# Retention and two gated layers on one core: parity by parity matmuls, an earlier scaling of chunk 4, tables in two parts

## The chip, the cores and the metric

One NeuronCore of a Trainium2 chip runs the whole program. The metric is the device time in microseconds (us) of one execution, from the first to the last instruction and what lies around them; shorter is better. The engines are TensorE (PE in the rows; PEld is its weight load), VectorE (DVE), ScalarE (ACT), GpSimd (POOL) and SyncE (SP, which issues most DMAs).

## The reference

Three stages follow one another. Inputs are float32; the output is [3072, 512].

```
state = gamma * state + k_t (outer) v_t          # 4 sequences, 8 heads, 768 steps, head size 64
y_t   = scale * q_t . state                      # gamma = 1 - 2^(-5-h), one for each head h
x     = y, heads side by side                    # [3072, 512]
h     = x @ w_in ; x = (h * sigmoid(1.702 h)) @ w_out            # 512 -> 2048 -> 512
x     = (sigmoid(x @ w_gate) * (x @ w_val)) @ w_out2             # 512 -> 1536 -> 512
```

The weights arrive in float64 and are turned into float32 on the core.

## The kernel before

**The recurrence as chunks.** The steps are cut into chunks of 128 (24 chunks, s = 0 to 23, six for each of four sequences; c = s mod 6). For each chunk the 8 heads are held as four pairs (`hp`), two parities each (`i`): parity 0 lies in partitions 0 to 63, parity 1 in 64 to 127. A chunk has four inputs of 256 KB, called Q, K, V and KN (k with time along the partitions). Its work is:

- `emit_qs(s)`: q times the decay table `dq_sb`, on POOL, L111. `emit_vs(s)`: v times the row `dv_sb[c]`, on POOL, L117.
- `emit_scores(s)`: eight float32 matmuls k.qs (L138), one for each parity and pair. A parity uses one half of the rows of the array and writes a PSUM bank of its own. After the four of one parity, DVE multiplies its bank with the triangle `tri` into `A` (L141).
- `emit_y(s)`: where c > 0 four matmuls with the state `R` (L173, the whole array); then eight matmuls of the values, vs.A (L180), again one for each parity and pair. Here a parity uses one half of the array's columns; both write the same bank, each its half of the partitions. DVE scales the bank by `dg_sb` (L186); then `halves()` takes it apart: ACT writes the upper part `xh` (L190), DVE the rest `xl` (L191).
- `emit_update(s)`, not where c = 5: eight matmuls kn.vs of half the width (L160) into the bank `st`, four for a parity, which again uses half of the columns. After each parity ACT copies its half of `st` into `R` (L165).

A float32 matmul of the program stands as two MATMUL records in the trace, so the eight matmuls of the scores are 16 records.

`burst(s)` runs emit_y(s), emit_update(s), emit_scores(s+1) and the halves of s, in that order on PE (for s = 3 there are no scores, and the halves come ahead of the update).

**The first gated layer.** `units` is the list of pieces (block of 512 tokens, slice of 128 hidden features). A unit i runs `proj` (12 matmuls of 512 columns, L262 to L264, into a bank "h"), `gated` (ACT sigmoid L272, DVE product L273; later units also ACT L278 and DVE L285), and `emit_out` of unit i-2 (L361 or L365 to L367). Bursts 0 to 3 run ahead of unit 0; bursts 4 to 23 are put into chosen units between the unit's `proj` and its `emit_out`. There are three "h" banks, taken in turn by `proj`, by emit_y and by the two parities of the scores. So in a burst of units the second bank of the scores is the one that the unit's own `proj` wrote, and it has to wait for L273; and the next `proj` takes the bank that emit_y wrote, and waits for `xl`.

**Weights.** `stage` issues DMAs of float64 tiles (L209, 512 KB each, four buffers), `convert` makes float32 of one: ACT L225 and L227, DVE L232 and L235, POOL L245. `split_for(i)` then makes the two parts wh (ACT L254) and wl (POOL L255; from unit 24 on DVE) that `proj` of unit i reads. Unit 0 and the bursts ahead of it need the first two of these.

**Order.** The body stands under a manual schedule: on every engine instructions run as the code emits them, and DMAs of the SP queue are issued in that order too, each waiting for its buffer. `load_next(s, ...)` loads inputs of a chunk into the pool `in_p` of 8 tiles. `dv_sb`, `dc_sb` and `dg_sb` are the small tables; DVE makes their later columns by multiplying the ones before (L693, 5 times, L695, 4 times).

The second gated layer (L390 on) follows and isn't touched.

Of the kernel before, what the change touches and what calls it, by code (L numbers as in the profile page):

```python
# [13 lines left out]
ALU = mybir.AluOpType  # L14

P = 128
D = 64
# [3 lines left out]
KC = DM // P  # L21
# [3 lines left out]
def retention_moe_moe2(  # L25
# [12 lines left out]
    nc = tc.nc  # L38
    NSTEP = qkv.shape[0]
    CPB = 6  # L40
# [36 lines left out]
    dv_sb = const.tile([P, CPB, H], F32, name="dv_sb")  # L77
    dc_sb = const.tile([P, H], F32, name="dc_sb")
    dg_sb = const.tile([P, CPB - 1, KC], F32, name="dg_sb")
# [10 lines left out]
    Q, K, V, KN = range(4)  # L90
# [8 lines left out]
    def load_next(s, *parts):  # L99
        for i in parts:  # L100
            if s < NSTEP and i not in in_t.get(s, {}):
                load_in(s, i, in_p, "in")

    qs_t, vs_t = {}, {}

    def emit_qs(s, engine=nc.gpsimd):

        if s < NSTEP:
            qs_t[s] = at_p.tile([P, KC, C], F32, name="qs", tag="qs")
            q = in_t[s][Q].rearrange("p (a i) -> p a i", a=KC)  # L110
            engine.tensor_tensor(out=qs_t[s], in0=q, in1=dq_sb, op=ALU.mult)  # L111
# [15 lines left out]
    def att_bank(name):  # L127
        banks.rotate(-1)
        return psum_tile(banks[-1], (P, 4, C))

    def emit_scores(s):

        k = in_t[s][K].rearrange("p (a j) -> p a j", a=KC)
        bank = [att_bank("sc") for _ in range(2)]
        for i in range(2):
            p = slice(D * i, D * (i + 1))
            for hp in range(KC):
                nc.tensor.matmul(bank[i][:, hp, :], k[p, hp, :], qs_t[s][p, hp, :], start=True, stop=True)  # L138
            A = a_p.tile([P, 4, C], F32, name="A", tag="A")
            A_t[s, i] = A  # L140
            nc.vector.tensor_tensor(  # L141
                out=A, in0=bank[i], in1=tri.unsqueeze(1).to_broadcast([P, KC, C]), op=ALU.mult
            )
# [3 lines left out]
    def emit_update(s):  # L147


        c = s % CPB  # L150
        if c == CPB - 1:
            return
        if c == 0:
            state[s // CPB] = psum_tile("st", (P, KC, P))
        st = state[s // CPB]
        kn, vs = in_t[s][KN], vs_t[s]
        for i in range(2):
            for hp in range(KC):
                h = 2 * hp + i
                nc.tensor.matmul(  # L160
                    st[D * i:D * (i + 1), hp, :D], kn[:, D * h:D * (h + 1)], vs[:, h, :],
                    start=(c == 0 and hp == 0), stop=True, skip_group_check=True,
                )
            a, b = D * i, D * (i + 1)
            nc.scalar.copy(R[(s + 1) % 2][a:b, :, a:b], st[a:b, :, :D])  # L165

    def emit_y(s):

        c = s % CPB
        bank = att_bank("y")  # L170
        if c > 0:
            for hp in range(KC):
                nc.tensor.matmul(  # L173
                    bank[:, hp, :], R[s % 2][:, hp, :], qs_t[s][:, hp, :],
                    start=(hp == 0), stop=False, skip_group_check=True,
                )
        for i in range(2):
            for hp in range(KC):
                h = 2 * hp + i
                nc.tensor.matmul(  # L180
                    bank[D * i:D * (i + 1), hp, :], vs_t[s][:, h, :], A_t[s, i][:, hp, :],
                    start=(c == 0 and hp == 0), stop=True, skip_group_check=True,
                )
        if c > 0:
            g = dg_sb[:, c - 1, :].unsqueeze(2).to_broadcast([P, KC, C])
            nc.vector.tensor_tensor(out=bank, in0=bank, in1=g, op=ALU.mult)  # L186
        xh, xl = (x[:, :, s % 4 * C:(s % 4 + 1) * C] for x in x_t[s // 4])

        def halves():
            nc.scalar.copy(xh, bank)  # L190
            nc.vector.tensor_tensor(out=xl, in0=bank, in1=xh, op=ALU.subtract)  # L191

        return halves
# [10 lines left out]
    def stage(n=1):  # L204

        for _ in range(min(n, len(to_stage))):
            ph, f, k = to_stage.popleft()
            t = cv_p.tile([P, 512], U64, name="w64", tag="w64", bufs=4)
            nc.sync.dma_start(out=t, in_=(w1 if ph == "1" else w2)[f, k])  # L209
            staged.append((ph, f, k, t))  # L210
# [81 lines left out]
    def burst(s):  # L292

        if s % 4 == 0:
            alloc_x(s // 4)
        halves = emit_y(s)
        if s == 3:
            halves()
        emit_update(s)
        if s + 1 < NSTEP and s != 3:  # L300
            emit_scores(s + 1)
        if s != 3:
            halves()
        for t in (in_t, qs_t, vs_t):
            t.pop(s, None)
# [351 lines left out]
    with tc.manual_schedule():  # L657
# [7 lines left out]
        for t in range(1, 4):  # L665
            for i in (Q, K, V, KN):
                load_in(t, i, wraw_p, "wraw")
                if (t, i) == (1, K):
                    nc.sync.dma_start(out=dg_sb[:, 0, :], in_=dg)
            if t != 2:  # L670
                stage()
        stage(2)
        load_next(4, Q, K, V, KN)
        nc.gpsimd.memset(tri, 1.0)
        nc.gpsimd.affine_select(
            out=tri, in_=tri, compare_op=ALU.is_ge, fill=0.0, base=0, pattern=[[1, C]], channel_multiplier=-1
# [12 lines left out]
        emit_scores(0)  # L689
        emit_vs(0)  # L690
        nc.vector.tensor_tensor(out=dc_sb, in0=dc_sb, in1=dc_sb, op=ALU.mult)
        for c in range(1, CPB):
            nc.vector.tensor_tensor(out=dv_sb[:, c, :], in0=dv_sb[:, c - 1, :], in1=dc_sb, op=ALU.mult)  # L693
        for c in range(1, CPB - 1):
            nc.vector.tensor_tensor(out=dg_sb[:, c, :], in0=dg_sb[:, c - 1, :], in1=dg_sb[:, 0, :], op=ALU.mult)  # L695
        first = second = None
        for t in range(4):
            if t < 3:
                emit_qs(t + 1)
            burst(t)  # L700
            if t == 0:
                load_next(5, Q, K, V, KN)
                first = convert(1)
                first[0]()
            elif t == 1:
                first[1]()
            elif t == 2:
                first[2]()
                second = convert(1)
                second[0]()  # L710
            if t < 3:
                emit_vs(t + 1)
            if t == 2:
                split_for(0)
        second[1]()
        second[2]()
        split_for(1)
        stage(2)
# [5 lines left out]
        for i, (b, f) in enumerate(units):  # L724
            if b == len(blocks1) - 1 and f == 0:
                assert not staged and not to_stage
                right.close()
                open_early()
                xs = prep_x(0)
                load_chain(0)  # L730
            first = staged and staged[0][0] == "1"
            conv, conv2 = ([lambda: None] * 3 for _ in range(2))
            if first:
                conv = convert(1)
                if i < FH:
                    conv2 = convert(1)
            elif staged and (5 * i) // 8 > (5 * (i - 1)) // 8:
                conv = convert(1)
            xh, xl = x_t[b]
            n = blocks1[b][1]  # L740
            if 0 < i < FH:
                split_for(i + 1)
            conv[0]()
            conv[1]()
            if i < FH:
                conv[2]()
            hb = psum_tile("h")
            proj(hb, w_t.pop((i, 0)), xh, xl, n)
            if i >= FH:
                split_for(i + 1)  # L750
            split_out(i + 1)
            if i == len(units) - 1:
                split_out(i + 2)
            g_t[i] = gated(hb, n, i < WHOLE)
            gated_lo(g_t[i], n)
            if i == 0:
                emit_qs(4)
                emit_scores(4)
                emit_vs(4)
                load_next(6, Q, K)  # L760
                emit_qs(5)
                banks.clear()
                banks.append("h")
            if i in bursts:
                burst_and_next(bursts[i])
            if i >= FH:
                conv[2]()
            stage(4 - len(staged))
            for step in conv2:
                step()  # L770
            pend.append(i)
            while pend and i - pend[0] >= DEPTH:
                emit_out(pend.popleft())
            next(xs, None)
            if b == len(blocks1) - 1:
                if f == 9:
                    sums(0)
                elif f in (11, 13):
                    split_chain(0, f == 13)()
# [144 lines left out]
```

## Time and profile before

| | us |
|---|---|
| three runs of the kernel: median (lowest to highest) | 1217.59 (1216.28 to 1217.83) |
| the execution that was profiled | 1216.4 |
| its span, first to last instruction | 1214.7 |
| PE busy in it | 1189.9 (98%) |
| DVE, ACT, POOL busy | 661.3, 573.5, 570.0 |

A row of a timeline gives the start in us from the span's start, the time from the first start to the last end, engine, line, operation, output<-inputs, their shapes and the count of merged instructions; in brackets the idle time of the engine just before, and what ended it. A MATMUL record is longer than the engine's time for it, since matmuls overlap in the pipeline: what one costs in a row of many is read from start to start. [...]

### The profile page before, as it was taken

What the parts mean: (1) busy time and instruction counts of PE and PEld (TensorE: products, weight loads), DVE (VectorE), ACT (ScalarE), POOL (GpSimd) and SP (SyncE); (2) the same over time, 40 slices, a digit from 0 to 9 for tenths busy, and PEclk for the clock granted to TensorE, in tenths of its full rate; (3) what the DMA queues carried; (4) which work ended last, traced back from release to release, by engine and by line L of the source; (5) the groups of instructions that cost most, each with busy time, mean ns of one, the idle gap of its engine ahead of it and who ended that gap; (6) DMA issues with size and microseconds to landing.
All of it is one profiled execution on the core that took longest, in us unless ns stands there. A gap on an engine that the chain in (4) does not pass through costs nothing.

```text
span 1214.7 us, 16082 instructions
## 1 busy us (share of the span) xinstructions
PE 1189.9 (98%) x5910; PEld 979.7 (81%) x5910; DVE 661.3 (54%) x904; ACT 573.5 (47%) x996; POOL 570.0 (47%) x443
## 2 busy tenths in 40 slices
PE   7799999999999999999999999999999999999998
PEld 7666888888888888888788888888888888888887
DVE  5665555455445544644565545458545458535454
ACT  3445664444555554545545534355535254625251
POOL 3665774434433543333455443438544348534340
PEclk9899999999999999999999999999999999999999
DMA  8565343633324434310300321114311123311111
GB/s 304 171 193 173 98 163 122 208 113 131 113 92 143 134 115 125 130 52 28 105 25 18 114 61 44 61 45 146 103 53 53 52 66 132 98 52 53 53 35 70
DMA packets 62431, 122.96 MB, mean 101 GB/s; under 512 B 6800, under 2 KB 16272, under 8 KB 62352
## 3 DMA queue, kind: packets, MB, share of 16 engines
q1 hardware_dynamic: 61632, 121.01, 30.6%
q8 instruction: 46, 0.75, 0.3%
q10 hardware_dynamic: 720, 0.92, 0.2%
q14 instruction: 33, 0.27, 0.1%
HBM read 97.79 MB, written 24.12 MB: 100 GB/s over the span
## 4 chain that ended last, share of the span: by engine, by line
PE 95%; DVE 1%; ACT 1%; DMA 1%; issue 0%; POOL 0%; SPq 0%; DVEq 0%; ACTq 0%; POOLq 0%
PE pa L512 16%; PE pd L512 8%; PE h L262 7%; PE h L264 7%; PE h L263 7%; PE acc L365 7%; PE acc L367 6%; PE acc L366 6%; PE po L636 4%; PE po L634 4%; PE po L635 4%; PE pb L512 4%; PE h L138 3%; PE acc L361 2%; PE h L180 2%; PE st L160 1%
## 5 line engine op out<-in xcount | busy, mean ns | idle before, releaser
L255 POOL TENSOR_TENSOR wl<-wraw,wh 128x512 fp32r<-128x512 f32 x112 | 154.1, 1381 | 293.8 <-ACT wh L254 279.7
L262 PE MATMUL h<-xh,wh 128*128 128x512 f32 x384 | 153.6, 400 | 1.6 <-DVE xl L191 1.5
L273 DVE TENSOR_TENSOR sg<-h,sg 128x512 f32<-128x512 f32 x88 | 60.8, 691 | 170.2 <-ACT sg L272 170.2
L264 PE MATMUL h<-xh,wl 128*128 128x512 f32 x384 | 149.8, 390 | 0.1
L263 PE MATMUL h<-xl,wh 128*128 128x512 f32 x384 | 149.8, 390 | 0.0
L365 PE MATMUL acc<-gh,wh 128*128 128x512 f32 x352 | 138.8, 394 | 0.0
L367 PE MATMUL acc<-gl,wh 128*128 128x512 f32 x352 | 137.1, 390 | 0.0
L366 PE MATMUL acc<-gh,wl 128*128 128x512 f32 x352 | 137.1, 389 | 0.0
L254 ACT CAST wh<-wraw 128x512 fp32r<-128x512 f32 x184 | 107.8, 616 | 38.6 <-PE acc L367 35.4
L504 POOL TENSOR_TENSOR ol<-raw,oh 128x768 fp32r<-128x768 f32 x36 | 66.9, 1859 | 124.7 <-ACT oh L501 124.7
L272 ACT ACTIVATE sg<-h 128x512 f32<-128x512 f32 x88 | 52.5, 597 | 131.7 <-PE h L264 131.4
L512 PE MATMUL pa<-xoh,oh 128*128 128x512 f32 x288 | 112.7, 391 | 0.2 <-ACT u L571 0.2
L512 PE MATMUL pa<-xol,oh 128*128 128x512 f32 x288 | 112.1, 389 | 0.0
L512 PE MATMUL pa<-xoh,ol 128*128 128x512 f32 x288 | 112.1, 389 | 0.0
L285 DVE TENSOR_TENSOR gl<-sg,gh 128x512 fp32r<-128x512 f32 x88 | 69.5, 790 | 60.4 <-ACT gh L278 60.4
L624 POOL TENSOR_TENSOR wol<-wor,woh 128x512 fp32r<-128x512 f32 x36 | 57.1, 1586 | 83.2 <-ACT woh L623 80.1
L278 ACT CAST gh<-sg 128x512 fp32r<-128x512 f32 x88 | 54.6, 621 | 71.3 <-DVE sg L273 71.3
L262 PEld LDWEIGHTS h<-xh,wh 128*128 128x128 f32 x384 | 72.3, 188 | 19.0 <-issue 3.3
L263 PEld LDWEIGHTS h<-xl,wh 128*128 128x128 f32 x384 | 72.4, 189 | 16.6 <-issue 1.9
L264 PEld LDWEIGHTS h<-xh,wl 128*128 128x128 f32 x384 | 72.3, 188 | 15.7 <-DVE wl L255 0.5
L634 PE MATMUL po<-woh,g2h 128*128 128x512 f32 x216 | 84.0, 389 | 0.0
L635 PE MATMUL po<-wol,g2h 128*128 128x512 f32 x216 | 84.0, 389 | 0.0
(136 smaller groups left out, 2622.6 us busy)
## 6 DMA issues: line engine op xcount, KB each, us to landing
w<-in_w_dram SPq DMA_DIRECT2D x68, 512.0 KB, 3.7
in_t<-in_qkv_dram SPq DMA_DIRECT2D x93, 256.0 KB, 4.0
raw<-w2d SPq DMA_DIRECT2D x72, 256.0 KB, 3.1
w2d<-cva SPq DMA_DIRECT2D x36, 256.0 KB, 2.2
wor<-w2d SPq DMA_DIRECT2D x36, 256.0 KB, 2.6
out_dram<-ost SPq DMA_DIRECT2D x23, 256.0 KB, 2.0
xt<-x2d SPq DMA_DIRECT2D x18, 256.0 KB, 4.4
x2d<-ost SPq DMA_DIRECT2D x14, 256.0 KB, 2.5
```

Source lines behind the costliest of these rows:

```text
L254: nc.scalar.copy(wh, raw)
L255: lo_engine.tensor_tensor(out=wl, in0=raw, in1=wh, op=ALU.subtract)
L262: nc.tensor.matmul(bank[:, :n], wh[:, k, :], xh[:, k, :n], start=(k == 0), stop=False)
L263: nc.tensor.matmul(bank[:, :n], wh[:, k, :], xl[:, k, :n], start=False, stop=False)
L264: nc.tensor.matmul(bank[:, :n], wl[:, k, :], xh[:, k, :n], start=False, stop=(k == KC - 1))
L285: nc.vector.tensor_tensor(out=gl[:, :n], in0=sg[:, :n], in1=gh[:, :n], op=ALU.subtract)
L365: nc.tensor.matmul(a, wh[:, wc], gh[:, :n], start=st, stop=False)
L366: nc.tensor.matmul(a, wl[:, wc], gh[:, :n], start=False, stop=False)
L367: nc.tensor.matmul(a, wh[:, wc], gl[:, :n], start=False, stop=sp)
L512: nc.tensor.matmul(bank, w[:, kk], x[:, k, :], start=start and k == 0 and w is wh and x is xh, stop=stop and k == 1 and w is wl, skip_grou ...
L634: nc.tensor.matmul(bank, gh, wh, start=f == 0, stop=False)
L635: nc.tensor.matmul(bank, gh, wl, start=False, stop=False)
```

## The change

Four edits, all in the code that makes the retention.

1. In `emit_scores`, in the values of `emit_y` and in `emit_update` the loops over parity and pair are exchanged: the matmuls alternate between the parities. The DVE products of the scores and the ACT copies of the update stand behind all eight matmuls of both parities.
2. `load_next(4, Q, K)` stands ahead of two weight loads that it followed, and V and KN of chunk 4 stay behind them.
3. `emit_qs(4)`, which stood in unit 0 behind its gating, stands ahead of the POOL step of the second weight tile.
4. The small tables: `dv_sb[1]` alone is made ahead of burst 0, columns 2 and 3 (with the first two of `dg_sb`) behind burst 0, and the last two (with the last two of `dg_sb`) behind burst 1.

```diff
@@ emit_scores
+        for hp in range(KC):
+            for i in range(2):
+                p = slice(D * i, D * (i + 1))
+                nc.tensor.matmul(bank[i][:, hp, :], k[p, hp, :], qs_t[s][p, hp, :], start=True, stop=True)
         for i in range(2):
-            p = slice(D * i, D * (i + 1))
-            for hp in range(KC):
-                nc.tensor.matmul(bank[i][:, hp, :], k[p, hp, :], qs_t[s][p, hp, :], start=True, stop=True)
             A = a_p.tile([P, 4, C], F32, name="A", tag="A")
@@ emit_update
-        for i in range(2):
-            for hp in range(KC):
+        for hp in range(KC):
+            for i in range(2):
                 h = 2 * hp + i
                 nc.tensor.matmul(
                     st[D * i:D * (i + 1), hp, :D], kn[:, D * h:D * (h + 1)], vs[:, h, :],
                     start=(c == 0 and hp == 0), stop=True, skip_group_check=True,
                 )
+        for i in range(2):
             a, b = D * i, D * (i + 1)
             nc.scalar.copy(R[(s + 1) % 2][a:b, :, a:b], st[a:b, :, :D])
@@ emit_y
-        for i in range(2):
-            for hp in range(KC):
+        for hp in range(KC):
+            for i in range(2):
                 h = 2 * hp + i
@@ the body
+        load_next(4, Q, K)
         stage(2)
-        load_next(4, Q, K, V, KN)
+        load_next(4, V, KN)
...
-        for c in range(1, CPB):
-            nc.vector.tensor_tensor(out=dv_sb[:, c, :], in0=dv_sb[:, c - 1, :], in1=dc_sb, op=ALU.mult)
-        for c in range(1, CPB - 1):
-            nc.vector.tensor_tensor(out=dg_sb[:, c, :], in0=dg_sb[:, c - 1, :], in1=dg_sb[:, 0, :], op=ALU.mult)
+        def factors(*cs):
+            for c in cs:
+                nc.vector.tensor_tensor(out=dv_sb[:, c, :], in0=dv_sb[:, c - 1, :], in1=dc_sb, op=ALU.mult)
+            for c in range(max(1, cs[0] - 1), cs[-1]):
+                nc.vector.tensor_tensor(out=dg_sb[:, c, :], in0=dg_sb[:, c - 1, :], in1=dg_sb[:, 0, :], op=ALU.mult)
+        factors(1)
...
             burst(t)
+            if t < 2:
+                factors(2 * t + 2, 2 * t + 3)
...
         second[1]()
+        emit_qs(4)
         second[2]()
...
-                emit_qs(4)
                 emit_scores(4)
```

On PE, burst 4 (in unit 1): the second half of the values, the update and the scores of chunk 5. The number at a name tells buffers apart; `[waits ...]` names the semaphores that the instruction waits for. Before:

```order
L180 MATMUL h_515<-A_463,vs_465 64x128 [waits DVE_49]
L180 MATMUL h_515<-A_463,vs_465 64x128 x3
L160 MATMUL st_244<-vs_465,in_t_185 64x64 [waits DMAHW3_49]
L160 MATMUL st_244<-vs_465,in_t_185 64x64 x3
L160 MATMUL st_244<-vs_465,in_t_185 64x64 [waits Activation_49]
L160 MATMUL st_244<-vs_465,in_t_185 64x64 x3
L138 MATMUL h_539<-qs_471,in_t_273 128x128 [waits DMAHW5_49,Pool_49]
L138 MATMUL h_539<-qs_471,in_t_273 128x128 x3
L138 MATMUL h_540<-qs_471,in_t_273 128x128 [waits DVE_49]
L138 MATMUL h_540<-qs_471,in_t_273 128x128 x3
```

The same place in the changed kernel, where these lines are L182, L161 and L138:

```order
L182 MATMUL h_515<-A_461,vs_465 64x128
L182 MATMUL h_515<-A_463,vs_465 64x128
L161 MATMUL st_236<-vs_465,in_t_185 64x64 [waits DMAHW3_49]
L161 MATMUL st_236<-vs_465,in_t_185 64x64 x7
L138 MATMUL h_539<-qs_471,in_t_269 128x128 [waits DMAHW5_49,Pool_49]
L138 MATMUL h_540<-qs_471,in_t_269 128x128 [waits DVE_49]
L138 MATMUL h_539<-qs_471,in_t_269 128x128
L138 MATMUL h_540<-qs_471,in_t_269 128x128
```

The wait for ACT in the middle of the update is gone, and the wait for DVE that stood in the middle of the scores stands at their second matmul.

On POOL, from the values of chunk 3 (vs, L117) through the two weight splits (wl) to the scaled q of chunk 5 (qs, L111). Before:

```order
L117 TENSOR_TENSOR vs<-in_t,dv_sb 128x512
L255 TENSOR_TENSOR wl<-wraw,wh 128x512
L245 TENSOR_TENSOR wraw<-cva,cvb 128x512
L255 TENSOR_TENSOR wl<-wraw,wh 128x512
L245 TENSOR_TENSOR wraw<-cva,cvb 128x512
L111 TENSOR_TENSOR qs<-in_t,dq_sb 128x512
L117 TENSOR_TENSOR vs<-in_t,dv_sb 128x512
L111 TENSOR_TENSOR qs<-in_t,dq_sb 128x512
```

The same place in the changed kernel (L247 and L257 are L245 and L255 of before):

```order
L117 TENSOR_TENSOR vs<-in_t,dv_sb 128x512
L257 TENSOR_TENSOR wl<-wraw,wh 128x512
L111 TENSOR_TENSOR qs<-in_t,dq_sb 128x512
L247 TENSOR_TENSOR wraw<-cva,cvb 128x512
L257 TENSOR_TENSOR wl<-wraw,wh 128x512
L247 TENSOR_TENSOR wraw<-cva,cvb 128x512
L117 TENSOR_TENSOR vs<-in_t,dv_sb 128x512
L111 TENSOR_TENSOR qs<-in_t,dq_sb 128x512
```

The scaled q of chunk 4 stands three instructions earlier, behind the first split instead of behind the second and a further weight tile.

## Rows read from the trace of the kernel before

**Rows 1.** The page: the chain that ended last, by engine.

```profile
PE 95%; DVE 1%; ACT 1%; DMA 1%; issue 0%; POOL 0%; SPq 0%; DVEq 0%; ACTq 0%; POOLq 0%
```

**Rows 2.** Waits of PE: us in total, times, longest.

```profile
PE st L160 <- ACT R L165: 11.1, 20, 1.6
```

**Rows 3.** Timeline of PE: one burst in a unit, from its values on.

```profile
217.06 1.25 PE L180 MATMUL h<-A,vs 128*64 128x128 f32 x13
...
218.15 0.27 PE L180 MATMUL h<-A,vs 128*64 128x128 f32 x1
218.16 0.28 PE L160 MATMUL st<-vs,in_t 128*64 128x64 f32 x2
...
218.37 0.27 PE L180 MATMUL h<-A,vs 128*64 128x128 f32 x1
218.39 0.34 PE L160 MATMUL st<-vs,in_t 128*64 128x64 f32 x3
219.19 0.68 PE L160 MATMUL st<-vs,in_t 128*64 128x64 f32 x8 [0.46 <-ACT R L165]
219.80 1.71 PE L138 MATMUL h<-qs,in_t 64*128 64x128 f32 x16
221.44 0.50 PE L365 MATMUL acc<-gh,wh 128*128 128x512 f32 x1
```

**Rows 4.** Timeline of PE: scores ahead of unit 0, parities in "acc" and "h".

```profile
17.80 0.82 PE L138 MATMUL acc<-qs,in_t 64*128 64x128 f32 x5
18.35 0.37 PE L138 MATMUL h<-qs,in_t 64*128 64x128 f32 x1
...
18.56 0.27 PE L138 MATMUL h<-qs,in_t 64*128 64x128 f32 x1
18.57 0.27 PE L138 MATMUL acc<-qs,in_t 64*128 64x128 f32 x1
...
18.79 0.72 PE L138 MATMUL h<-qs,in_t 64*128 64x128 f32 x5
19.43 1.16 PE L173 MATMUL acc<-qs,R 128*128 128x128 f32 x8
```

**Rows 5.** Timeline of PE: units 0 and 1.

```profile
30.25 0.40 PE L263 MATMUL h<-xl,wh 128*128 128x512 f32 x1
...
32.57 0.39 PE L264 MATMUL h<-xh,wl 128*128 128x512 f32 x1
37.84 3.09 PE L138 MATMUL acc<-qs,in_t 64*128 64x128 f32 x16 [4.88 <-POOL qs L111]
40.87 0.79 PE L262 MATMUL h<-xh,wh 128*128 128x512 f32 x1
...
44.63 1.05 PE L173 MATMUL h<-qs,R 128*128 128x128 f32 x8
...
51.58 0.47 PE L262 MATMUL h<-xh,wh 128*128 128x512 f32 x1 [1.52 <-DVE xl L191]
```

**Rows 6.** Stretches: us, busy PE, PEld, DVE, ACT, POOL (count), clock, DMA.

```profile
33.30:51.50 18.20, 11.76 (x84) 10.28 (x84) 10.08 (x15) 8.04 (x16) 12.02 (x10) 0.81 0.53 179
36.00:42.80 6.80, 4.96 (x21) 4.35 (x22) 2.48 (x5) 1.75 (x3) 4.01 (x4) 0.50 0.38 116
```

**Rows 7.** Timelines of POOL and DVE in the first 35 us.

```profile
23.30 1.04 POOL L117 TENSOR_TENSOR vs<-in_t,dv_sb 128x512 f32<-128x512 f32 x1
...
32.87 1.27 POOL L255 TENSOR_TENSOR wl<-wraw,wh 128x512 fp32r<-128x512 f32 x1 [0.73 <-ACT wh L254]
...
9.30 1.73 DVE L693 TENSOR_TENSOR dv_sb<-dv_sb,dc_sb 128x8 f32<-128x8 f32 x5
```

**Rows 8.** Timeline of DVE and PE behind the scores of a burst.

```profile
204.62 1.29 DVE L141 TENSOR_TENSOR A<-h,tri 128x512 f32<-128x512 f32 x2 [1.35 <-PE h L138]
205.82 0.68 DVE L191 TENSOR_TENSOR xl<-h,xh 128x512 fp32r<-128x512 f32 x1
...
207.92 0.39 PE L262 MATMUL h<-xh,wh 128*128 128x512 f32 x1
```

## The prediction

> **What bounds the kernel now.** I read the chain of work that ended last first: PE makes up 95% of it [rows 1], so a time that PE doesn't need is a time saved, as long as nothing else is late next. Then PE's waits [rows 2]: 20 times it stood in the middle of an update, until ACT had copied the first parity's half of `st`, 11.1 us in all, the longest 1.6. Next to that there is one idle stretch of 4.88 us before the scores of chunk 4, which waited for POOL's scaled q [rows 5]. Then the timeline of one burst, start to start [rows 3]: 217.06 to 219.80 for values and update (2.74 us), 219.80 to 221.44 for the scores (1.64).
>
> The row that matters most shows that PE can work on both halves of the array at once. In [rows 4] the scores of one parity ("acc") start at 17.80, the second parity ("h") at 18.35, when the first has some records left. From there on the two run side by side: "h" at 18.56, "acc" at 18.57. A single parity needs the same time for each record: five take 0.72 - 0.27 = 0.45 us from first to last start, 0.11 each. The same holds for halves of columns [rows 3]: a value of the second parity starts at 218.15, an update of the first at 218.16. So today each parity runs alone for about half of its time, since the other stands behind it in the queue, and the overlap is found only at the border.
>
> **Scores.** If both parities run together from the first matmul, the set lasts as long as one parity alone: from 18.35 to the next kind of matmul at 19.43, 1.08 us [rows 4], instead of 1.64 [rows 3]. That is 0.56 saved. Bursts 5 to 22 make 18 such sets: **10.1 us**. The two DVE products can no longer start while PE is on the second parity, which costs PE nothing while a unit's output matmuls follow (see the second rival).
>
> **Values and update.** A record of the values takes 0.11 (218.15 to 218.37 is two of them), the first a little more: 0.93 for the eight of a parity. An update takes 0.06 (a group of two lasts 0.28, one of three 0.34), a parity of eight 0.68 - 0.22 = 0.46 from first to last start, and the scores start 0.15 later [rows 3]. Together 0.93 + 0.46 + 0.15 = 1.54 instead of 2.74: 1.20 saved. Of this 0.62 comes from the order alone: the last update of the first parity starts at 218.39 + 0.12 = 218.51, the first of the second at 219.19, 0.68 where 0.06 would do. ACT's two copies now stand behind the update; who reads `R` is the next burst, a unit or more later. The burst shown waited 0.46; the mean of the 19 without the longest is (11.1 - 1.6) / 19 = 0.50 [rows 2], so 0.04 more. Bursts 6 to 22 without 11 and 17 are 15: 15 x 1.24 = **18.6 us**. Bursts 5, 11, 17 and 23 have values only: 217.06 to 218.37 + 0.11 is 1.42, minus 0.93 is 0.49; 4 x 0.49 = **2.0 us**.
>
> **The start, up to projection 2** (L262 at 51.58 [rows 5]), is worked out in three steps, since other engines are late there.
>
> Ahead of unit 0, PE alone would gain some 6 us in bursts 0 to 3 (three sets of scores and four updates, by the prices above, with the longest wait of 1.6). But DVE's products and weight steps lie between, and the values of chunk 3 need `vs`, which ran at 23.30 to 24.34 [rows 7] behind a weight tile on POOL. Of the tables' edit, four of the five dv_sb products (1.73 us for five, 0.35 each [rows 7]) and four smaller ones move from a time when DVE waited to places behind `xl` of bursts 0 and 1; I bound that between 0 (DVE waits there too) and 2 us. I take 3 us of gain, between 1 and 5.
>
> The scores of chunk 4 then find q ready: its POOL instruction stands ahead of one that waited for DVE, and K of chunk 4 is loaded before two weight tiles that nobody reads until unit 0. Projection 0 goes on at 0.232 a matmul (30.25 to 32.57 is ten) and ends at 32.80; the scores take 1.08; projection 1 can start at 33.9 instead of 40.87: 7.0. Its third matmul needs `wl`, done at 32.87 + 1.27 = 34.14 [rows 7], just in time. [...]
>
> So PE would be 11 us ahead at 44.63, and burst 4 would add its own 1.8 and the wait of 1.52 for `xl`. There I let DVE decide: it had 10.08 us of work between 33.30 and 51.50 [rows 6], the queue up to `xl` of chunk 4, and starts on it about 3 us earlier, at 30.3. Without any pause it is through at 40.4, and projection 2 starts at 40.6 instead of 51.58: 11. DVE waits for PE once or twice on the way, and PE idles while it waits, which may bring the lower clock back: I take **10 us**, between 6 (four or five us of such pauses) and 13 (the first step at its best).
>
> **The sum.** 10.1 + 18.6 + 2.0 + 10 = 40.7. The profiled execution took 1216.4, which gives 1175.7; it lies 1.2 under the median of the runs, so on the median's footing 1177. Its own range is 1169 to 1184: the start between 6 and 13, and 3 us either way on the bursts.
>
> [...] Records of the second parity start ahead of remaining ones of the first, and column halves run together [rows 3, 4]. [...]
>
> **The rivals.**
>
> *Half of the overlap.* PE looks only some records ahead (the second parity began 0.55 us after the first [rows 4]), and the alternating order may fill it less well, since each program matmul is two records. Half of what comes from running side by side: scores 5, values and updates 9.9 by order plus half of 8.7, values alone 1, start 9.5: 29.8, or 1188. Chance 0.13.
>
> *DVE is late in every burst.* The next projection needs the bank that `xl` empties. Today `xl` ends at 205.82 + 0.68 = 206.50, the projection starts at 207.92 [rows 8]: 1.4 us of room. The products start about as long after the first score as before, but PE is 0.56 quicker through the scores, so some 0.8 stays; work of DVE ahead of the burst can eat that. At 0.5 us lost in each of 20 bursts: 10, or 1187. Chance 0.09.
>
> *Column halves don't alternate well.* Then values and updates run one after the other: 16 x 0.11 + 16 x 0.06 with the ends is 2.91, 0.13 worse than today after the wait is gone; values alone 0.39 worse. 10.1 - 2.0 - 1.6 + 9 = 15.5, or 1202. Against it stand the pairs in [rows 3]. Chance 0.04.
>
> *Nothing overlaps in the new order.* The scores too are then 0.34 worse than today, since the overlap at the border is lost: -6.1 - 2.0 - 1.6 + 8.5 = -1.2, or 1219: no change. Chance 0.03.
>
> *The change of half costs time.* The first record of a parity is 0.10 longer than the others (0.37 against 0.27 [rows 4]), a first update about 0.05. If each change of half paid that, and nothing ran side by side, scores lose 1.1, values with update 0.9, values alone 0.7: 18 x 1.1 + 15 x 0.9 + 4 x 0.7 = 36, and the start gains only about 4: 1250. There are 18 x 8 + 15 x 16 + 4 x 8 = 416 changes in these bursts, so from about 0.01 us a change, without overlap, it is slower. Against it: in [rows 4] the halves change with every record between 18.56 and 18.79, and pay nothing. Chance 0.04.
>
> **How the numbers follow.** The forecast has 0.67, the rivals 0.13, 0.09, 0.04, 0.03, 0.04. The range 1168 to 1191 takes in most of the forecast's own and of the first two rivals, which hold 0.89 together; their tails are left out. What a measurement can tell from no change is about 0.2% (2.4 us): faster 0.93 (the forecast and the first three rivals), same 0.03, slower 0.04.
>
> **What would show it.** Right: L138 starting in pairs, 1.1 us from the first score to what follows; no wait of PE for ACT in the update; 1.5 us from the first value to the first score; scores of chunk 4 right behind projection 0, and the lower clock gone from 36 to 43. Wrong: score records 0.11 apart one by one; new waits of PE for `xl`, for L273's bank or for the second `A`; a start that gains less than 6 us because DVE or POOL waits in another place.

## The result, and the profile after

| | before | after |
|---|---|---|
| median of four runs, us (lowest to highest) | 1217.57 (1216.28 to 1217.83) | 1179.18 (1178.35 to 1180.15) |
| ratio to before (95% interval) | | 0.9687 (0.9670 to 0.9704) |
| the profiled execution, us | 1216.4 | 1179.18 |
| its span, us | 1214.7 | 1177.5 |

38.4 us were saved where 40.7 had been forecast; 1179.2 lies 2 us above the forecast of 1177 and inside the range. In the changed kernel L138 is still the scores and L142 their DVE product (L141 before); L182 are the values (L180), L161 the update (L160), L167 its copies (L165), L175 the matmuls with the state (L173), L264 to L266 the projection, L363 and L367 on the output, L192 `xh` (L190), L193 `xl` (L191), L275 the product of the gating (L273), L234 and L237 the DVE steps of a weight (L232, L235).

The chain that ended last, by engine, answers to [rows 1]: PE is still what counts.

```profile
PE 96%; DVE 1%; DMA 1%; ACT 1%; issue 0%; POOL 0%; SPq 0%; DVEq 0%; POOLq 0%; ACTq 0%
```

The waits of PE after (us in total, times, longest) answer to [rows 2]. The 20 waits for ACT's copy are gone, and so is the one of 4.9 us for POOL's scaled q [rows 5]. The longest is new, the second stood there before with 1.52 [rows 5]; they and all others of the list lie ahead of 43 us.

```profile
PE h L138 <- DVE gw L275: 2.6, 1, 2.6
PE h L264 <- DVE xl L193: 1.7, 1, 1.7
...
PE h L264 <- ACT xh L192: 1.0, 1, 1.0
...
PE h L182 <- POOL vs L117: 0.9, 1, 0.9
```

The timeline of PE after, the first two pairs of a set of scores ahead of unit 0 (beside [rows 4]), one burst in a unit (beside [rows 3]), and units 0 to 2 (beside [rows 5]):

```profile
16.59 0.37 PE L138 MATMUL acc<-qs,in_t 64*128 64x128 f32 x1
16.60 0.37 PE L138 MATMUL h<-qs,in_t 64*128 64x128 f32 x1
16.80 0.27 PE L138 MATMUL acc<-qs,in_t 64*128 64x128 f32 x1
16.81 0.27 PE L138 MATMUL h<-qs,in_t 64*128 64x128 f32 x1
...
189.15 1.09 PE L182 MATMUL h<-A,vs 128*64 128x128 f32 x16
190.07 0.64 PE L161 MATMUL st<-vs,in_t 128*64 128x64 f32 x16
190.64 1.16 PE L138 MATMUL h<-qs,in_t 64*128 64x128 f32 x16
191.73 0.50 PE L367 MATMUL acc<-gh,wh 128*128 128x512 f32 x1
...
26.99 0.51 PE L265 MATMUL h<-xl,wh 128*128 128x512 f32 x1 [0.22 <-DVE xl L193]
...
29.72 1.16 PE L138 MATMUL acc<-qs,in_t 64*128 64x128 f32 x16
30.81 0.50 PE L264 MATMUL h<-xh,wh 128*128 128x512 f32 x1
...
33.83 1.05 PE L175 MATMUL h<-qs,R 128*128 128x128 f32 x8
...
39.46 1.80 PE L138 MATMUL h<-qs,in_t 64*128 64x128 f32 x14 [2.61 <-DVE gw L275]
42.92 0.76 PE L264 MATMUL h<-xh,wh 128*128 128x512 f32 x1 [1.66 <-DVE xl L193]
...
47.48 3.59 PE L363 MATMUL acc<-gw,wraw 128*128 128x512 f32 x8
```

Two things are to be seen. The parities start 0.01 us apart, pair after pair, and a burst takes 1.49 us from the first value to the first score and 1.09 us for the scores, where [rows 3] had 2.74 and 1.64. And in unit 1 PE stands twice, for the bank that L275 has to empty and for `xl`; projection 2, at 42.92, then needs 47.48 - 42.92 = 4.56 us.

To part the two halves of the change I use the first output matmul of all: it starts at 54.43 before and at 47.48 after. What lies ahead of it (bursts 0 to 4, units 0 and 1, projection 2) is called the start, the rest of the span the bursts' part. The row of that first output matmul before, in the timeline of PE:

```profile
54.43 3.59 PE L361 MATMUL acc<-gw,wraw 128*128 128x512 f32 x8
```

So the start gave 6.95 us, and the part behind it (1214.7 - 54.43) - (1177.5 - 47.48) = 30.25, together 37.2 us. The medians differ by 38.4, since the profiled execution before lay 1.2 us below its median and the one after on it.

### The profile page after: what moved, and what is told of

Read it like the earlier page. It is cut to its first block, busy times and chain, and to the rows that moved or that the text cites. A ratio compares the mean times of both kernels' runs of the same rounds, so it can differ in the third digit from the quotient of the medians.

```text
span 1177.5 us, 16083 instructions
## 1 busy us (share of the span) xinstructions
PE 1163.4 (99%) x5910; PEld 952.7 (81%) x5910; DVE 660.5 (56%) x904; ACT 574.7 (49%) x996; POOL 570.8 (48%) x443
## 3 DMA queue, kind: packets, MB, share of 16 engines
q1 hardware_dynamic: 61632, 121.01, 31.2%
## 4 chain that ended last, share of the span: by engine, by line
PE 96%; DVE 1%; DMA 1%; ACT 1%; issue 0%; POOL 0%; SPq 0%; DVEq 0%; POOLq 0%; ACTq 0%
PE pa L514 17%; PE pd L514 8%; PE h L266 7%; PE h L264 7%; PE h L265 7%; PE acc L367 7%; PE acc L369 7%; PE acc L368 7%; PE po L636 4%; PE po L638 4%; PE pb L514 4%; PE po L637 4%; PE acc L363 2%; PE h L138 2%; PE h L182 2%; PE pd L636 1%
## 5 line engine op out<-in xcount | busy, mean ns | idle before, releaser
L257 POOL TENSOR_TENSOR wl<-wraw,wh 128x512 fp32r<-128x512 f32 x112 | 154.2, 1382 | 265.3 <-ACT wh L256 250.1
L264 PE MATMUL h<-xh,wh 128*128 128x512 f32 x384 | 154.1, 401 | 2.7 <-DVE xl L193 1.7
L275 DVE TENSOR_TENSOR sg<-h,sg 128x512 f32<-128x512 f32 x88 | 60.9, 692 | 160.7 <-ACT sg L274 160.7
L266 PE MATMUL h<-xh,wl 128*128 128x512 f32 x384 | 150.5, 392 | 0.1
L367 PE MATMUL acc<-gh,wh 128*128 128x512 f32 x352 | 138.9, 395 | 0.0
L264 PEld LDWEIGHTS h<-xh,wh 128*128 128x128 f32 x384 | 72.6, 189 | 20.7 <-issue 3.9
L266 PEld LDWEIGHTS h<-xh,wl 128*128 128x128 f32 x384 | 72.5, 189 | 16.9 <-DVE wl L257 1.4
```

Of the source, the lines that this page charges most:

```text
L257: lo_engine.tensor_tensor(out=wl, in0=raw, in1=wh, op=ALU.subtract)
L264: nc.tensor.matmul(bank[:, :n], wh[:, k, :], xh[:, k, :n], start=(k == 0), stop=False)
L266: nc.tensor.matmul(bank[:, :n], wl[:, k, :], xh[:, k, :n], start=False, stop=(k == KC - 1))
L367: nc.tensor.matmul(a, wh[:, wc], gh[:, :n], start=st, stop=False)
```

## The experiments

The start and the part behind it, in the profiled execution of each kernel, worked out in that way. A start is read from one execution each, and it depends on when in it the granted clock (TensorE's, as a share of its full speed) fell and rose: projection 2 took 2.85 us at 1.00 before, and 4.56 after, 0.50 up to 46.60. So 1 or 2 us between two starts can be the clock's, and e5 started late beside that (see there); the part behind is steadier (1129.9 to 1130.1 for the four kernels with edit 1 whole and nothing changed behind unit 1). The edits are shown shortened.

| kernel | median us | first output matmul at | span behind it |
|---|---|---|---|
| before | 1217.6 to 1217.8 | 54.43 | 1160.3 |
| after | 1179.18 | 47.48 | 1130.0 |
| e1_alternate_only | 1182.66 | 52.23 | 1130.1 |
| e2_start_only | 1211.51 | 49.68 | 1160.3 |
| e3_update_order | 1204.99 | 55.64 | 1148.2 |
| e4_scores_only | 1206.69 | 53.85 | 1151.1 |
| e5_values_only | 1213.81 | 58.57 | 1156.6 |
| e12_values_update | 1191.02 | 49.82 | 1138.8 |
| e10_by_two | 1181.03 | 47.76 | 1131.9 |
| e6_qs4_late | 1182.74 | 52.39 | 1130.0 |
| e7_tables_at_once | 1179.43 | 47.52 | 1129.9 |
| e8_unit1_free | 1177.32 | 43.77 | 1132.5 |
| e9_vs3_ahead | 1180.22 | 42.91 | 1135.5 |
| e11_units1_3_free | 1177.93 | 42.79 | 1133.5 |

### The two halves apart

**e1_alternate_only**: the kernel before with edit 1.

```diff
-        for i in range(2):
-            for hp in range(KC):
+        for hp in range(KC):
+            for i in range(2):     # scores, values, update; products and copies behind all eight
```

> The kernel before with the alternation of parities and the copies behind the update (edit 1), and nothing else. Theory of the prediction: the bursts from projection 2 on give the whole 30 us; ahead of it the bursts 0 to 3 give about 3, the idle stretch before the scores of chunk 4 and the lower clock behind it stay, burst 4 gives 1.8: 1182 to 1183. Rival (the other edits carry a good part of the gain): over 1190. Rival (the edits are worth nothing): 1179.

1182.66, as the theory had it: ratio 0.9702 (0.9673 to 0.9730). The part behind the start is that of the whole change, to 0.1 us. The start gave 2.2 and kept its idle stretch; the granted clock was 0.50 twice in it, from 34.8 to 41.5 us and from 48.4 to 51.7 (matmuls of 512 columns 0.43 us apart there, 0.23 elsewhere), where before it was so once in units 0 and 1 [rows 6]. Waits of PE in it:

```profile
PE acc L138 <- POOL qs L111: 5.3, 1, 5.3
PE h L264 <- DVE xl L193: 2.1, 1, 2.1
```

**e2_start_only**: the changed kernel with edit 1 undone.

```diff
-        for hp in range(KC):
-            for i in range(2):
+        for i in range(2):
+            for hp in range(KC):   # all three places, products and copies inside
```

> The changed kernel with edit 1 undone, so only the earlier scaling of chunk 4 and the tables in two parts. Theory: the idle stretch of 4.9 us closes and projection 1 runs at the upper clock, worth 8, but DVE then decides when projection 2 starts, which leaves 4 to 7: 1211 to 1214. Rival (DVE doesn't hold it): 1209.5. Rival (the gap moves as a whole to another wait): 1217.

1211.51, ratio 0.9939 (0.9919 to 0.9960), within the theory's range; behind the start nothing changed. By medians the two gains add up to 35.2 + 6.3 = 41.5, 3 us more than the 38.4 of the change; in the profiled executions the starts add up exactly, 2.20 + 4.75 = 6.95. The 3 us lie within the intervals of the two ratios, so that the two halves get in each other's way is not shown.

### What the alternation is made of

**e3_update_order**: only the copies behind both parities; parity by parity as before.

```diff
         for i in range(2):
             for hp in range(KC): ...        # update
-            nc.scalar.copy(R[(s + 1) % 2][a:b, :, a:b], st[a:b, :, :D])
+        for i in range(2):
+            nc.scalar.copy(R[(s + 1) % 2][a:b, :, a:b], st[a:b, :, :D])
```

> The kernel before with one thing changed: in the update all matmuls of both parities come first, parity by parity as before, and the two copies behind them. Theory: only the wait goes, 0.66 a burst in 15 bursts is 9.9, and 1 to 3 in the first five: 1205 to 1207. Rival (most of the burst gain came from the order and not from side by side): 1195 or less.

1204.99, at the lower end of the theory's range, and not for its reasons alone: behind the start it gave 12.1, where 9.9 was expected, and the start lost 1.2. The clock can account for that loss: it was 0.50 from 34.2 to 44.4 us and again from 51.3 to 54.6, under projection 2 (its matmuls 0.43 us apart), where before it was 1.00 (0.23 apart). PE in burst 4:

```profile
46.03 1.25 PE L181 MATMUL h<-A,vs 128*64 128x128 f32 x13
...
48.01 1.71 PE L138 MATMUL h<-qs,in_t 64*128 64x128 f32 x16
```

That is 1.98 from values to scores instead of 2.74: 0.76 where 0.62 to 0.66 was worked out. Without the wait the second parity's updates follow the first's in one row (11 records in a group at 47.36, 0.72 us long, where [rows 3] had three, the wait, and eight), so that their border can overlap as well; the sum had left that out.

**e4_scores_only**: only the scores alternate (the first hunk of the diff).

> The kernel before with the scores alone alternating. Theory: 0.56 in 18 bursts is 10.1, and 1 to 2 at the start: 1205 to 1207. Rival (later products of DVE make the next projection wait): 1210 or more, with waits of PE for xl in the units.

1206.69, as expected: 9.2 behind the start, near the 10.1 of the sum. The wait for `xl` stands in unit 1 alone, as before, and grew from 1.5 to 2.1 us; in the units behind it, where output matmuls follow a burst, none came.

**e5_values_only**: only the values alternate (halves of the columns).

> The kernel before with the values alone alternating (halves of the columns). Theory: the values of both parities take 0.93 instead of 1.42, but the update of the first parity no longer overlaps with their end, so that a burst with update gains 0.1 and the four bursts without one 0.5 each: 1213 to 1216. Rival (column halves don't run side by side in alternating order): values one after the other, 0.8 longer in 15 bursts and 0.4 in four: 1230.

1213.81, as the theory had it, and far from the rival's 1230. A burst, on PE:

```profile
204.11 1.09 PE L180 MATMUL h<-A,vs 128*64 128x128 f32 x16
205.03 0.63 PE L160 MATMUL st<-vs,in_t 128*64 128x64 f32 x8
206.11 0.68 PE L160 MATMUL st<-vs,in_t 128*64 128x64 f32 x8 [0.45 <-ACT R L165]
206.72 1.71 PE L138 MATMUL h<-qs,in_t 64*128 64x128 f32 x16
```

All 16 records of the values take 0.92 to the first update, so halves of the columns run side by side when they alternate. But a burst is 2.61 instead of 2.74: the overlap that was found at the border between values and update is lost again, and the gain appears only when the update alternates too. This profile starts late (58.57), and its rows show PE at about half speed until some 20 us: 48 MATMUL records between 12.20 and 20.20, where before had 82, at a granted clock of 1.00 in both. What slowed it, they don't show. The eight matmuls with the state behind the second set of scores, before and in e5:

```profile
13.97 1.16 PE L173 MATMUL acc<-qs,R 128*128 128x128 f32 x8
...
17.18 2.07 PE L173 MATMUL acc<-qs,R 128*128 128x128 f32 x8
```

So I judge it by the part behind the start: 3.7 us.

**e12_values_update**: values and update alternate, the copies stand behind.

> The kernel before with values and update alternating and the copies behind; scores as before. Theory: 1.24 in 15 bursts and 0.49 in four is 20.6, and 1 to 2.5 at the start: 1194 to 1196. Rival (the pieces add up: e5 alone gave 4 and the order alone 13): 1201.

1191.02, 3 us faster than expected. The bursts' part is 21.5, near the 20.6 of the theory; what was wrong is the start, 4.6 instead of 1 to 2.5. With e4's 9.2 the pieces make 30.7, beside the 30.3 of the whole change. A burst without an update, on PE:

```profile
56.97 1.09 PE L181 MATMUL h<-A,vs 128*64 128x128 f32 x16
57.99 1.71 PE L138 MATMUL h<-qs,in_t 64*128 64x128 f32 x16
```

The same burst before:

```profile
61.58 1.58 PE L180 MATMUL h<-A,vs 128*64 128x128 f32 x16
63.09 1.71 PE L138 MATMUL h<-qs,in_t 64*128 64x128 f32 x16
```

That is 1.02 from values to scores instead of 1.51, and their difference is the 0.49 of the sum. The start is ahead of e1's although e1 has more: in e12 the clock was 0.50 once, from 32.9 to 39.6 us, and projection 2 ran at 1.00 (its matmuls 0.23 us apart).

**e10_by_two**: two matmuls of a parity, four records, at a time.

```diff
-        for hp in range(KC):
-            for i in range(2):
+        for g in range(2):
+            for i, hp in ((i, 2 * g + j) for i in range(2) for j in range(2)):
```

> The changed kernel with the parities alternating after every two matmuls (four records) instead of after every one. Theory (PE starts the other half's record when it stands four behind the one that runs, as at the border in the kernel before): still side by side, within 0.2 us a set: 1179 to 1183. Rival (it needs a neighbour in the queue): half of the overlap is lost, 1188 or more.

1181.03: 1.9 us more than after, so nothing like half of the overlap was lost. PE in a set of scores ahead of unit 0:

```profile
16.93 0.37 PE L138 MATMUL acc<-qs,in_t 64*128 64x128 f32 x1
16.95 0.37 PE L138 MATMUL h<-qs,in_t 64*128 64x128 f32 x1
...
17.48 0.27 PE L138 MATMUL acc<-qs,in_t 64*128 64x128 f32 x1
17.49 0.37 PE L138 MATMUL h<-qs,in_t 64*128 64x128 f32 x1
17.59 0.27 PE L138 MATMUL acc<-qs,in_t 64*128 64x128 f32 x1
17.70 0.27 PE L138 MATMUL h<-qs,in_t 64*128 64x128 f32 x1
17.70 0.27 PE L138 MATMUL acc<-qs,in_t 64*128 64x128 f32 x1
```

A record that stands four behind the first in the queue starts 0.02 after it. In [rows 4] the second parity stood eight behind, and began with the fifth record. In both, then, the record that started on the free half lay four behind the running one; that the old order overlapped only at its borders agrees with it. A set takes 1.19 instead of 1.09: one slot of 0.1 is lost (17.59 to 17.70 has one record where two could be).

### What the start is made of

**e6_qs4_late**: the changed kernel with edits 2 and 3 undone.

```diff
-        load_next(4, Q, K)
         stage(2)
-        load_next(4, V, KN)
+        load_next(4, Q, K, V, KN)
-        emit_qs(4)              # ahead of second[2]()
+                emit_qs(4)      # in unit 0, ahead of emit_scores(4)
```

> The changed kernel with the loads of chunk 4 and its scaled q back in their old places; alternation and tables stay. Theory: the idle stretch before the scores of chunk 4 is back, about 5 us, but as DVE decides the start of projection 2 anyway, most of it was not worth its length: 1182 to 1184. Rival (the earlier q is worth its whole gap of 8): 1187.

1182.74: the earlier q is worth 3.6 us by medians, not its gap of 8. PE waits 5.2 again, but projection 2 starts only some 5 us later, at 47.98 in the profiled execution.

**e7_tables_at_once**: the changed kernel with edit 4 undone.

```diff
-        factors(1)
+        for c in range(1, CPB): ...          # all of dv_sb
+        for c in range(1, CPB - 1): ...      # all of dg_sb
-            if t < 2:
-                factors(2 * t + 2, 2 * t + 3)
```

> The changed kernel with edit 4 undone: the tables are made at once ahead of burst 0. Theory (DVE waits at either place, and later queues decide): 1178.5 to 1180.5, no change against 1179.2. Rival (in two parts it frees DVE for the products of burst 1): 1181. Rival (the parts hold up DVE ahead of the first weight tile in burst 1, which the values of chunk 3 wait for): 1177.5 to 1178.

1179.43 beside 1179.18, first output matmul at 47.52 beside 47.48: the tables in two parts change nothing.

**e8_unit1_free**: the changed kernel; in unit 1 the weight's DVE and POOL steps behind the burst, the halves of chunk 4 ahead of the scores.

```diff
+            if i != 1:
                 conv[1](); conv[2]()         # ahead of the projection
...
                 burst_and_next(bursts[i])
+            if i == 1:
+                conv[1](); conv[2]()
...
+        if s == 4:
+            halves()
         emit_scores(s + 1)
```

> The changed kernel, in unit 1 alone: the DVE and POOL steps of that unit's weight conversion stand behind burst 4 instead of ahead of the projection, and the halves of chunk 4 stand ahead of the scores of chunk 5. Theory (DVE's queue holds the bank of the scores and xl, and the idle time that follows brings the lower clock): the wait of 2.61 for L275 shrinks to under 1, that of 1.66 for xl too, projection 2 starts 2.5 to 3.5 earlier and runs at the upper clock (1.7 more): 1174 to 1175.5. Rival (the lower clock comes all the same): 1176 to 1177. Rival (the conversions that are moved are late for units 2 and 3): 1179 or more.

1177.32, ratio to before 0.9665 (0.9648 to 0.9681); neither the theory's 1174 to 1175.5 nor a rival's story. PE:

```profile
37.32 1.16 PE L138 MATMUL h<-qs,in_t 64*128 64x128 f32 x14 [0.60 <-DVE gw L275]
39.36 0.47 PE L264 MATMUL h<-xh,wh 128*128 128x512 f32 x1 [0.88 <-DVE xl L193]
...
54.44 1.16 PE L138 MATMUL h<-qs,in_t 64*128 64x128 f32 x14 [2.00 <-DVE gw L275]
```

The theory of DVE's queue holds: the two waits fell from 2.61 and 1.66 to 0.60 and 0.88, projection 2 starts at 39.36 instead of 42.92, the first output matmul 3.7 us earlier. But 2.5 of it is given back behind the start, of which the wait of 2.00 in unit 3: the steps that were moved now stand ahead of L275 there. The lower clock came too, for 3.4 us (stretch, then busy PE, PEld, DVE, ACT, POOL with counts, granted clock, DMA share, GB/s):

```profile
39.90:43.30 3.40, 3.40 (x9) 2.64 (x8) 3.33 (x5) 0.00 (x0) 2.25 (x3) 0.50 0.80 277
```

Behind the longer wait, that of 2.00, it stayed at 1.00 (43.40 to 60.00 us). And in e9 and e11, which hold the same two moves and show the same waits of 0.60 and 0.88 in unit 1 (0.01 us apart), it stayed at 1.00 through projection 2 (its matmuls 0.23 us apart, in e8 0.43 during the fall). So whether the clock falls here differs from one execution to the next.

**e9_vs3_ahead**: e8, with `emit_vs(3)` ahead of `first[2]()`.

> The kernel of e8, and the scaled v of chunk 3 ahead of the POOL step of the first weight tile. Theory: PE's wait of 0.89 for it goes, then the second product A is last: 0.7 less than e8. Rival (the weight tile is what counts): the same as e8.

1180.22, 2.9 us slower than e8, where 0.7 faster was expected. The wait for `vs` of chunk 3 did go. Its first output matmul is 0.9 earlier, which the clock accounts for (projection 2 took 2.83 us at 1.00, where e8 took 4.41, for 3.4 of them at 0.50), but 3.0 are lost behind it. Two of its waits of PE, which e8's list doesn't have, are for the low parts of weights:

```profile
PE h L266 <- POOL wl L257: 1.5, 2, 1.2
```

The longer one stands in projection 3, at 48.19. The rest is the clock again, which fell behind the wait in unit 3 in this execution:

```profile
55.40:58.70 3.30, 3.30 (x16) 2.27 (x15) 2.25 (x5) 2.95 (x6) 2.75 (x3) 0.50 0.37 137
```

There the second part of the scores and the output matmuls behind it, 1.16 and 3.70 long in e8, took 1.97 and 4.51, 1.6 us more. These rows account for the profiled execution, 2.1 us slower than e8's. That the median is 2.9 slower they don't settle, nor whether moving `vs` is what makes the clock fall there.

**e11_units1_3_free**: e8 with the same two moves in unit 3.

```diff
-            if i != 1:
+            if i not in (1, 3):
-        if s == 4:
+        if s in (4, 5):
```

> e8 with the same two moves in unit 3 as well: its DVE and POOL steps of the weight conversion behind burst 5, the halves of chunk 5 ahead of the scores of chunk 6. Theory (in e8 the moved steps stand ahead of L275 in unit 3, and PE waits 2.00 there): that wait goes, 1175 to 1176. Rival (the steps are only passed on to unit 5): 1177 to 1178, with a wait of the scores there.

1177.93: no better than e8. The wait of 2.00 in unit 3 is gone (the scores there took 1.66 us where e8 had 3.56), and others came, 1.25 us for a weight and 0.81 for the bank in unit 5:

```profile
48.10 0.50 PE L266 MATMUL h<-xh,wl 128*128 128x512 f32 x1 [1.25 <-POOL wl L257]
...
69.55 1.16 PE L138 MATMUL h<-qs,in_t 64*128 64x128 f32 x14 [0.81 <-DVE gw L275]
```

The wait in unit 5 is the one that the rival named: the work moved out of unit 3 is in part passed on. The 1.25 is not of these moves, since e9, which has none in unit 3, shows 1.23 at the same place; it came in the two executions whose projection 2 ran at the full clock, so the time that the clock gives back there is lost again to `wl`. e8 and e11 are 1 to 2 us under the changed kernel by medians; the intervals of the ratios overlap, so that they beat it is likely and not shown.

## Why the prediction was right, point by point

**The three terms of the bursts.** Scores take 1.09 for a set where 1.08 was forecast, values with update 1.49 where 1.54 was. Values alone gave the 0.49 forecast, though both lengths are 0.09 longer than worked out there (1.51 and 1.02): the step from the last value to the scores was taken too short in both. Together 30.25 us came behind the start where the three terms had 30.7. Added up burst by burst, the rows give 9.8, 19.4 and 2.0, in all 31.2; the 0.9 that is missing is spread over the projections, and what costs it is open. e4 and e12 show the two parts one by one, and e3 and e5 that for values and update both the order and the side by side are needed: the order alone gave 0.76 a burst, the values side by side alone 0.13, all together 1.25.

**The start, first step.** The second matmul of projection 0 moved from 30.25 to 26.99: 3.3, with 3 taken. Its bound was the one named, `vs` of chunk 3, with two more behind it: PE waits 0.9 for `vs` of chunk 3, then for `xh` and `xl`. The tables, bounded by 0 to 2 us, cost nothing (e7).

**Second step.** Scores right behind projection 0 at 29.72, projection 1 at 30.81 instead of 40.87: 10.1 with 10 forecast, and burst 4 at 33.83 instead of 44.63: 10.8 with 11. That 11 has 1.0 in it for a faster projection 1, which no run shows: it took 33.83 - 30.81 = 3.02 us at a granted clock of 1.00, where it had taken 44.63 - 40.87 = 3.76 [rows 5], so 0.74.

**Third step: the term that was mis-sized.** DVE does decide when projection 2 starts, but at 42.92 and not at 40.6 to 41.6. So the term of 10 us, to the start of projection 2, was 51.58 - 42.92 = 8.66. And the lower clock, which the forecast left to its lower bound, came in projection 2, so that the whole start gave 6.95. The granted clock and DVE's work stand in these stretches (columns as in [rows 6]):

```profile
30.60:42.80 12.20, 8.05 (x74) 6.45 (x70) 11.20 (x15) 8.03 (x16) 10.35 (x9) 0.88 0.62 206
39.80:46.60 6.80, 5.14 (x23) 4.10 (x20) 5.69 (x8) 3.35 (x6) 5.64 (x6) 0.50 0.80 245
```

DVE was busy 11.2 of 12.2 us, where [rows 6] had 10.08 for the same queue: 1.1 more, and a pause of 0.88 for the scores. The forecast took the queue's work as given; two of its weight steps had become longer (1.66 us instead of 0.69, and 1.01 instead of 0.42; see the last section). PE stood 2.61 and 1.66 for it, and from 39.80 to 46.60 the clock was at its lower level; projection 2 took 4.56 instead of 54.43 - 51.58 = 2.85, 1.7 more. With 1.3 later by DVE that is the 3 us by which the sum was too high. The lower bound of 6 for this term, which the range took in, held. One of the signs that were to show the forecast wrong came, in unit 1 alone: a new wait for L273's bank (L275 now); the wait for `xl`, which the start was to gain, stayed. And the lower clock was not gone, it stood 4 us later. In e7 and e10, which share this start, the clock was 0.50 in the same place (matmuls of projection 2 0.43 us apart in both).

**Some luck in the total.** On the footing of the profiled executions the forecast was 1175.7 and 1179.2 was measured, 3.5 us too few; 2 us by the medians are left because the profiled execution before happened to lie 1.2 us under its median. The forecast's own range of 1169 to 1184 mixes these two footings: on the median's it would begin at 1171. That changes nothing in the outcome.

**The rivals.** Half of the overlap, no overlap, a price for each change of half: the pairs in the rows after speak against all three. That DVE is late in every burst: in a unit the room is still there. After (DVE, the burst at 189, and the next projection on PE):

```profile
191.83 1.29 DVE L142 TENSOR_TENSOR A<-h,tri 128x512 f32<-128x512 f32 x2
193.04 0.68 DVE L193 TENSOR_TENSOR xl<-h,xh 128x512 fp32r<-128x512 f32 x1
...
194.59 0.39 PE L264 MATMUL h<-xh,wh 128*128 128x512 f32 x1
```

`xl` ends at 193.72, and the next projection starts at 194.59: 0.87 of room, 0.8 expected, 1.4 before [rows 8]. It was late in one burst, that of unit 1. That column halves don't alternate well: e5 answers it with 0.92 us for 16 records.

## What to carry to other kernels

Where small matmuls use a half of the array each, write them alternating between the halves, and let no copy stand between the two: for values and update here the order gave 0.76 us a burst, the values side by side alone 0.13, and all together 1.25. When a large gap of the main engine is closed, add up the queue of the next engine over the whole stretch (here DVE, 10 us of work where PE was to gain 11) before counting the gap as gained. And read the granted clock behind each idle stretch that remains, in more than one execution: in this kernel it fell to 0.50 after a wait of 2.61 us; after waits of 0.60 and 0.88 it fell in one of three executions, and after one of about 2 us in e9 and not in e8.

## What the runs showed of the hardware that was not expected

**Which record starts on a free half.** A record that stood four behind in the order of the program started on the free half of the array at once (e10, 0.02 us apart), one that stood eight behind did not (0.55 later [rows 4]). Halves of columns ran side by side as well (16 records of the values in 0.92 us, e5). The records of the two halves don't start in the order of the program: in [rows 4] all eight of the first parity ("acc") stand ahead of the second's, and at 18.57 one of them starts behind one of the second ("h", 18.56).

**DVE's weight step has two durations.** In the changed kernel the same instruction took 0.69 and 1.66 us (DVE, unit 0):

```profile
31.69 0.69 DVE L237 SCALAR_TENSOR_TENSOR cva<-w,cva 128x512 uint32<-128x512 uint32 x1
...
35.14 1.66 DVE L237 SCALAR_TENSOR_TENSOR cva<-w,cva 128x512 uint32<-128x512 uint32 x1
```

At 31.69 POOL stood idle from 31.38 to 32.53; at 35.14 it was in this (POOL):

```profile
34.78 1.47 POOL L111 TENSOR_TENSOR qs<-in_t,dq_sb 128x512 f32<-128x512 f32 x1
```

This holds for the whole trace: of the 68 records of L237, 11 begin while POOL is in an instruction, and all 11 took 1.63 to 1.67 us; the other 57 took 0.69 to 0.70, also the 11 of them beside which a POOL instruction begins later. Before it is 12 records of L235 at 1.64 to 1.67, and 56 at 0.69.

All 11 came second, behind an instruction of POOL that had begun, and the one at 35.14 ends 0.55 us behind POOL's; what makes them longer, the rows don't show. Of the 1.1 us by which DVE's queue grew in the third step, this accounts: one record more at 1.66 than before, and one of L234 at 1.01 instead of 0.42 (at 34.10, beside POOL's `vs`). Where the q is late, the same two are short: before, L232 took 0.42 at 41.58 and L235 0.69 at 42.03, with POOL idle from 40.01 to 42.87. On DVE in e6, with the q late again:

```profile
39.53 0.69 DVE L237 SCALAR_TENSOR_TENSOR cva<-w,cva 128x512 uint32<-128x512 uint32 x1
```

So moving POOL's q also changed which DVE instructions it meets, and that made DVE's queue longer.
